# A written-out order of 1281 jobs, ordered anew, with other first loads and earlier idle matmuls

## The chip, the cores and the metric

The kernel runs on one core of one Trainium2 chip. Five engines work side by side, each through a queue of its own in order: PE (matrix products; its weight loads are listed apart, as PEld), DVE, ACT and POOL (elementwise work and copies), and SP, which only issues DMAs (ACT issues a few too). They wait for each other through semaphores. The metric is device time in microseconds; the kernel before took 269.9 us (median of three runs, 268.41 to 270.17).

## The reference

Two blocks in a row, all in float32, cut to what is computed:

```python
# attention with sketched features: q, k, v are (4 batches, 4 heads, 1088, 32), S1 and S2 are (8, 32)
a = einsum('rd,bhsd->bhsr', S1, x); b = einsum('rd,bhsd->bhsr', S2, x)
phi(x) = outer(a, b)                      # 64 features a row
kv, z = sums over s of phi(k) * v and of phi(k)
x = phi(q) @ kv / (phi(q) . z + 1e-6)     # becomes (4, 1088, 128)
# experts' attention: 4 experts, each row uses its best two
w, topk = softmax of the two largest of x @ w_gate
for e in experts:
    a = causal softmax of (x wq[e]) (x wk[e]).T / 8
    out += share of e in a row * (a @ (x wv[e]) @ wo[e])
```

S1 and S2 arrive as 64-bit floats and are turned into 32-bit ones on the chip.

## The kernel before

The program is a list of jobs (1281 of them, numbered as they are declared), each a small function that issues the instructions of one step on one engine. `Plan.run` goes through `ORDER`, a list of job numbers, and calls each; every engine gets its instructions in that order, and a letter behind a number picks the first or second engine of a job that can run on either (for a pair of idle matmuls the second choice is to leave it out). Buffers of a pool are handed out in the same order, so the list also settles which buffer a job gets, and with it whose release it waits for. No scheduler changes anything afterwards. A job waits for what it reads and for its buffer's last users.

**Start.** S1 and S2 are loaded (L235) into a tile that DVE has cleared first (job `room`, L238), decoded on DVE (L304 to L317) and copied to the other partitions by POOL, ACT and DVE (`spread`, L320). Batch 0's k comes in two halves by columns (L422, one on SP's queue and one on ACT's), its q in four pieces by head (L428), its v in four pieces (L435), which ACT copies into place (L445). DVE transposes k (L475) and q (L481). `sketch` (L510) multiplies k or q by the tables on PE; DVE transposes the result back (`back`, L514), and DVE or POOL multiplies out the 64 features (`features`, L524). `sums` (L566) is phi(k) against v. Jobs `dummy` (L249) are pairs of idle matmuls on a tile `idle` of zeros that DVE sets (L242); nobody reads what they give.

**Batch 0** then transposes q's features on PE (`turn qf`, L602), copies them (`keep qf`, L193), multiplies by the sums and divides (L628, L637). **Batches 1 to 3** do it the other way round: q's table is extended by the sums (`fifth`, L704), the features are scaled first, transposed on DVE (`turn f`, L741), and `numer` (L763) gives x already turned; ACT or DVE copies it (`keep x`), DVE turns it for the store.

**Experts.** `logits` (L814 or L820), `choose`, `shares` (L881 to L889, eight small operations on POOL) and masks fetched by DMA pick two experts a row. Per batch there are three groups of rows (of 6, 6 and 5 tiles of 64 rows). For a group PE makes the queries (L1002), DVE picks the chosen ones (L1015), and each of its tiles then runs through a chain: `score` on PE (L1040), `take` on DVE (L1052, adds the mask and finds the maximum), `exp` on ACT (L1068), `guard` (adds 1e-9; ACT L1074 or POOL L1076), `invert` on DVE (L1079), `weigh` on POOL (L1083), `turn A` on DVE (L1088). The `sum` jobs of the group (L1116) need all its tiles turned; then come copies, masks (`spread V` on POOL, L1143) and the output products (L1237, L1187, L1213). Batches overlap: batch b+1's preparation runs between batch b's groups.

Most copies can run on ACT or DVE, feature products on DVE or POOL, guards on ACT or POOL; the letters in `ORDER` choose.

The list is walked like this:

```python
for word in order:
    n, a = (int(word[:-1]), "ab".index(word[-1])) if word[-1] in "ab" else (int(word), 0)
    j = self.jobs[n]
    ...
    if j["eng"][a] != "-":
        for h in j["holds"]:
            if h not in self.where:
                self.where[h] = free[h[0]].popleft()
        j["f"](j["eng"][a])
```

Of the kernel before, what the change touches and what calls it, by code (L numbers as in the profile page):

```python
# [23 lines left out]
111 109a 107a 403 114a 113a 58 115 57 116a 407 121 404 63 122a 400 119 117 402 120a 406 405 118b 123 410 131 124 411  # L24
412 127 125 401 68 126a 132 128 135 151 152 133 11b 409 157 413a 129 415a 136 158 160 69 70 134a 130a 691 137 185 414a
184 188a 189a 153 154 155 163 156 161 416b 162a 172 690 173 14b 187 190 186 418 417 175 164a 191 159 213 688 199 408
419a 214 167 206 200 168 25b 220 215 421 207 689 420 208 422 221 209a 176 699 7b 423b 216a 192 201 138 227 193 169
425a 222 210 426 424a 174 170 202b 171b 223a 141 194 251 228 195a 250 211 252 217 6b 229 218 230a 255a 224 179 698 196
219 197 254a 427 177 253 429 180 225 198 203 71 178 212 16b 204 428 231 256 165 257 166a 72 34b 323 324 328a 296 430
226 140 435 142 232 327a 181 436 431 437 233 433a 272 329 432a 439a 13b 273 73 182 297 274 205 298 265 39b 280 281 266  # L30
258 282 275 139 694 434 259 695 326 299 267 276b 325 692 146 300b 234 438a 183a 330 301 235 277 283 284b 285 440 302
268a 702 705 703 144 278 236 148 303 237a 286 238a 240a 241 441 706a 260 288 442a 289 287 356 279 269 704a 710a 443a
242 363 261a 709a 290 364 270 271 239a 697 262 355 291 347 365 708a 461 707a 348 292a 357 5b 462 30b 701 263 696 366
693 340 367 42b 143 984 23b 244 358 293 368 27b 294 339 264 349 711 712 465 359a 18b 369a 295 150 341 463 464 145 304
305 983 350 243 370 351a 713a 466 700 306 987 371 360 352 307 342 308 147 715 467 353 444 447 361 714 354 372 309 719a
716 310b 477 718b 313a 471 311a 343a 312a 717b 314 315 362 344 476 468 720 316 990 721 331 332 480a 722 333 317 723
481a 482 479 319 334 478 724 446 448 729 483 345 320 318 491 335b 336 725 337 484 492 445 321a 485 469 543 512 346 338
542 547a 505 545 544 985 982 506 513 472 486 487a 986 488 727a 730 726a 507 473 373 374 731 375 546a 733a 450 548 376
549 732b 474 498 493 519 494a 377 475b 149 449 514 378 379 993 380 381 495 508b 520 499 515a 500 501a 382a 988 728 496
509 521 451 516 489 992 517 384a 454 734 735 989 518 510 502 383b 385b 386 387 736a 490 572 573 389 503 452 522a 737a  # L40
588 996 994 574 453 504 523 245 497 247 589 511 999 524 564 997 388 565 550 991 1000b 590 551 617 618 552 591 470 246
525 566 998a 616 557 1002b 248a 615 575 620a 558 1004a 567 755 1001b 559 592b 1003a 1006 619b 593 756 553a 457 621 757
622 758 568b 1005 594 322 759 455 460 569 765 595 554 570 576a 526 527 528 531a 648 571 760 647 577 761 530a 555 1007a
560b 532b 578 535 561 529a 649 390 632 533 581 391 631 556 580 562 658 534 563 582 655 536 656 583 650 249 459 458 623
1008 633 624 584b 634 579 585 651a 766 657 639 456 586 659 625 762 771 640 770 773 772 587 641 596 775a 774a 652 738
767 653 768 660 635b 776 777 661a 597 598 626 642 1009 1012a 662 636 654 599 663 600 392 627a 601 1013a 1010 637 664
638 643b 995 740 602a 603b 1011a 785 644 786 628 629 813 606 814 741 537 645 604a 806 607 630 605a 807 1014 778 609
539 538 739 646 1015 608 779 665 1016 780 666 540b 1017 667 1018 742 1023 808 781a 668 669 1024 32b 815 1025 787 670
671 394 816b 745 672 1019 673 792 836 21b 1021b 788b 1020b 746 674a 809a 817 541 1026a 763 1027b 837 769b 393 818 1022
675a 793 819 26b 840a 678 782 677b 612 810 611 841b 794 676a 744 783 838 752 679 1028 610 811 839 680 795b 681 799  # L50
613a 796 842 789 29b 843 1029 800 784 851 909 910 797 812 790 1031a 866 867 801 802b 791 743 1030b 852 853 914a 868
803 883 882 804 859 798 854b 858 874 884 875 805 764 860 10b 885 913b 861 876 869 844 886b 845 1049 862a 1050 911 912
877 863 915 820 846 855 878a 847a 1051 916 1052 864 848 870b 748 887 879 614 821 871 822 865 824b 823a 826a 1054 825a
849 888 889 682 942 880 872 941 36b 827 850 856 1053 933 828 683 829 881 934 949 873 750 935 925 1055 926 943 950 927
944 918 951 952 830 686 687 1135 857 945b 946 1136 928 395 917 953 954 1140b 1139b 831 1057 936 947 955a 1138 919 832
1137 920 747 754 921b 929a 1141 890 1032 937a 930 956 1142 922 891 938 923 939 685 931 948 749 1059 833 957 1182 1033
1181 834a 892 924 940 893 932 1183 1036 958 894 895 899a 684 897a 898b 1035 959 896a 753 960 961 962 963 901 1143 751
1144 19b 1145 964 965 900 1184 902 1060 966 967 1034 970b 903 1040 969b 968a 1061 1185b 971a 1150 1166 1165 1151 1041
1146b 973 1152 1158 972 974 1157 43b 1153a 1154 1173 1062 1147 1208 1167 1174 1211 1168 1209 1169a 975 1063a 1213a 9b
1186 1212a 1210 1039 1058 1175 33b 1187 1159 1170 1214 1056 1065 1066 1148 1064 1171 904 1188 1149 40b 1176 44b 906  # L60
835 1160 1069a 1177b 1037 1155 1068b 1215 1161b 1162 905 1070 1217 1045 1156 1178 907a 1172 1216 1240 1163 1179 1218
1219 1067 1180 1241 1048 1220a 1071 1164 1224 1225 1249 1233 1248 1242 1072 1221 1226 1227 908 1250 1228a 1251 1232
1252 12b 1229 1038 1243 1073 1222 1244a 1223 1234 1230 1043 1245 976 31b 1107 1108 1235 1044 977 1253 1042 1189 1246
979 1247 1109 1236a 1254a 1237 1231 1110a 1238 1190 1255 1191 1093 1086 1239 1094 1087 1192 1256 1257 980 1193 1074
28b 1100 1111 1088 1101 1095 1079 1080 1194 1258 1197a 1089b 1198a 1196b 1112 1081 1075a 1096b 1097 1082a 1259 978
1090 1260 1047 1102 1103a 1261 1262 35b 1046 1195b 1076 1077 1091 24b 1104 1263 1264 981 1083 1200 1105 1113 1098 1092
20b 1265 1199 1266 1270a 1201 1084 1267a 1106 1202 1078 1203 1204 1099 1268b 38b 1205 1085 15b 1269b 1272 1206a 1114
1115 1116 1207 1117a 1273 1271 1122 1121b 1274 1275 1119 1120a 1118 1125 1276 1123 1126 1127 1124b 1128 41b 1280 1278
1133b 1279 1277 1129a 1130b 1134a 1131b 1132a
""".split()  # L70


# [1254 lines left out]
```

## Time and profile before

| | us |
|---|---|
| median of 3 runs (lowest, highest) | 269.9 (268.41, 270.17) |
| the profiled execution | 270.48 |
| its span, first to last instruction | 268.8 |
| mean granted clock of PE in it | 0.993 |

The profile is one execution. Its page gives busy time by engine, the span in 40 slices, DMA queues, and the chain of work that ended last; the trace behind it answers for single instructions, windows and waits. Of the groups of instructions, the costliest by engine (line, engine, operation, output and inputs, size and count, then busy us and mean ns, then idle time ahead of them and who ended it):

```profile
L1083 POOL TENSOR_SCALAR w<-w,rs,sh 128x640 f32<-128x640 f32 (+16 forms) x68 | 55.6, 824 | 43.4 <-DVE rs L1079 40.2
L1068 ACT ACTIVATE w<-w,mx 128x576 f32<-128x576 f32 (+16 forms) x68 | 52.3, 770 | 58.4 <-DVE mx L1052 56.9
L1040 PE MATMUL pair<-xT,qs 128*128 128x384 f32 (+11 forms) x216 | 74.0, 480 | 0.0
```

A matmul in float32 shows as two instructions. The granted clock is recorded where it changes; ahead of the first record a window shows 1.00 whether or not that held.

### The profile page before, as it was taken

Reading aid. Unit: us, or ns where it says so; the run is one execution under the profiler, and the core shown is the slowest. Engines: PE = TensorE matmul, PEld = TensorE weight load, DVE = VectorE, ACT = ScalarE, POOL = GpSimd, SP = SyncE. Lnnn points to the kernel's source line nnn. Section 1 sums busy time; section 2 is a strip of 40 time slices with the busy share of each in tenths; the row PEclk is TensorE's granted clock in tenths of the full one; section 3 lists DMA queues with packets and bytes.
Section 4 is the critical chain, followed back from the end, with each engine's and each line's share of the span. In section 5 each row is a group of like instructions: output and inputs, shape, how many; then the busy total and the mean of one; then the engine's idle time right before and its main releaser. Section 6 shows DMA issues by size and latency. Waiting matters only on the chain.

```text
span 268.8 us, 9515 instructions
## 1 busy us (share of the span) xinstructions
PE 254.9 (95%) x3960; PEld 189.6 (71%) x3961; DVE 212.2 (79%) x550; ACT 102.6 (38%) x275; POOL 150.8 (56%) x246
## 2 busy tenths in 40 slices
PE   0889999989999999999999999999999999999994
PEld 0368576644887785876587996585789766689994
DVE  3687899997989888788999689899991379986343
ACT  2213655536622515252472323551701363354110
POOL 4276348999459944547555836166272594352741
PEclk9999999979999999999999999999999999999999
DMA  7938559990238677513441094402670458321012
GB/s 160 188 68 195 115 115 215 186 165 11 45 83 167 165 131 118 154 30 98 108 67 29 6 229 87 111 4 50 149 140 20 99 133 204 54 50 30 5 32 54
DMA packets 87739, 27.36 MB, mean 102 GB/s; under 512 B 58576, under 2 KB 87056, under 8 KB 87696
## 3 DMA queue, kind: packets, MB, share of 16 engines
q1 hardware_dynamic: 85184, 26.11, 48.1%
q10 hardware_dynamic: 2512, 0.64, 1.2%
q8 instruction: 31, 0.51, 0.9%
q14 instruction: 12, 0.10, 0.2%
HBM read 22.22 MB, written 4.52 MB: 100 GB/s over the span
## 4 chain that ended last, share of the span: by engine, by line
PE 77%; DVE 1%; issue 0%; DVEq 0%
PE pair L1116 28%; PE pair L1040 23%; PE pair L1002 8%; PE pair L1237 7%; PE pair L1187 3%; PE pair L763 2%; PE pair L566 2%; PE pair L510 2%; PE pair L1213 1%; PE pair L814 1%; DVE fp L741 0%; DVE w L514 0%; PE pair L704 0%; PE pair L698 0%; DVE ob L193 0%
## 5 line engine op out<-in xcount | busy, mean ns | idle before, releaser
L1083 POOL TENSOR_SCALAR w<-w,rs,sh 128x640 f32<-128x640 f32 (+16 forms) x68 | 55.6, 824 | 43.4 <-DVE rs L1079 40.2
L1068 ACT ACTIVATE w<-w,mx 128x576 f32<-128x576 f32 (+16 forms) x68 | 52.3, 770 | 58.4 <-DVE mx L1052 56.9
L1040 PE MATMUL pair<-xT,qs 128*128 128x384 f32 (+11 forms) x216 | 74.0, 480 | 0.0
L1052 DVE CUSTOM_DVE_ANT_0 w<-pair,mask 128x768 f32<-128x768 f32 (+14 forms) x68 | 48.2, 726 | 17.6 <-PE pair L1040 16.2
L1040 PEld LDWEIGHTS pair<-xT,qs 128*128 128x128 f32 x216 | 38.3, 190 | 25.4 <-issue 10.9
L1088 DVE STREAM_TRANSPOSE AT<-w 128x384 f32<-128x384 f32 (+15 forms) x68 | 50.4, 758 | 1.3 <-POOL w L1083 1.1
L1143 POOL TENSOR_TENSOR agg<-agg,mb 128x768 f32<-128x768 f32 (+1 forms) x22 | 34.1, 1559 | 20.2 <-ACT agg L193 7.0
L1116 PEld LDWEIGHTS pair<-AT,xra 32*128 32x128 f32 x1136 | 41.7, 185 | 4.4 <-issue 2.4
L1116 PE MATMUL pair<-AT,xra 32*128 32x160 f32 (+5 forms) x1136 | 44.7, 303 | 0.0
L1002 PE MATMUL pair<-xT,Mq 128*128 128x384 f32 (+1 forms) x96 | 34.3, 475 | 0.0
L193 ACT COPY agg<-pair 128x384 f32<-128x384 f32 (+1 forms) x31 | 13.4, 467 | 42.4 <-PE pair L1116 39.9
L524 POOL TENSOR_TENSOR fp<-w 128x576 f32<-128x576 f32 (+1 forms) x21 | 24.8, 1198 | 8.3 <-DVE w L514 8.0
L1116 PE MATMUL pair<-AT,xrb 32*128 32x160 f32 (+5 forms) x752 | 27.8, 288 | 0.0
L1116 PEld LDWEIGHTS pair<-AT,xrb 32*128 32x128 f32 x752 | 26.6, 185 | 1.5 <-issue 1.4
L1002 PEld LDWEIGHTS pair<-xT,Mq 128*128 128x128 f32 x96 | 17.2, 190 | 10.2 <-issue 2.5
L1015 DVE COPY_PREDICATED qs<-mb,pair 128x768 f32<-128x768 uint16 (+1 forms) x24 | 23.1, 964 | 0.8 <-ACT qs L193 0.4
L1237 PEld LDWEIGHTS pair<-Mo,agg 128*128 128x128 f32 x168 | 20.5, 192 | 3.1 <-issue 0.5
L1237 PE MATMUL pair<-Mo,agg 128*128 128x128 f32 x168 | 21.2, 277 | 0.0
L1076 POOL TENSOR_SCALAR rs<-zs 128x1 f32<-128x1 f32 x27 | 6.7, 249 | 17.9 <-ACT w L1068 13.4
L193 DVE COPY agg<-pair 128x384 f32<-128x384 f32 (+1 forms) x15 | 7.6, 516 | 10.8 <-ACT agg L193 5.9
L514 DVE STREAM_TRANSPOSE w<-pair 128x576 f32<-128x576 f32 (+2 forms) x18 | 12.1, 696 | 4.1 <-PE pair L510 3.8
L1139 DVE COPY_PREDICATED agg<-mb,pair 128x384 f32<-128x384 uint16 (+1 forms) x24 | 12.8, 547 | 1.1 <-ACT agg L193 1.0
(169 smaller groups left out, 292.5 us busy)
## 6 DMA issues: line engine op xcount, KB each, us to landing
xra<-xd SPq DMA_DIRECT2D x16, 192.0 KB, 4.4
xrb<-xd SPq DMA_DIRECT2D x16, 192.0 KB, 4.6
xrc<-xd SPq DMA_DIRECT2D x16, 160.0 KB, 4.1
mb<-md SPq DMA_DIRECT2D x4, 576.0 KB, 5.8
mb<-md SPq DMA_DIRECT2D x4, 480.0 KB, 5.0
mb<-md SPq DMA_DIRECT2D x6, 288.0 KB, 5.2
in<-in_k_dram SPq DMA_DIRECT2D x12, 136.0 KB, 3.9
in<-in_q_dram SPq DMA_DIRECT2D x3, 544.0 KB, 6.1
```

Source lines behind the costliest of these rows:

```text
L193: (nc.scalar.copy if eng == "ACT" else VEC[eng].tensor_copy)(o, i)
L524: VEC[e].tensor_tensor(out=f, in0=a[:, :, None, R : 2 * R].to_broadcast([128, j1 - j0, R, R]), in1=a[:, :, 0:R, None].to_broadcast([128, j ...
L1002: nc.tensor.matmul(plan[ps[x]][:, y, 0:w], Mq[:, ((1, 2), (0, 3))[x][y]], plan[xT][:, 64 * t0 : 64 * t1], start=True, stop=True)
L1015: nc.vector.copy_predicated(chosen(), rows(c), rows(plan[ps[x]]))
L1040: nc.tensor.matmul(plan[p][:, y, 0 : c1 - c0], plan[qs][:, 128 * t : 128 * t + 128], plan[xT][:, c0:c1], start=True, stop=True)
L1052: nc.vector.tensor_tensor_reduce(out=o, in0=src, in1=msk, scale=-1.0, scalar=mx[:, b, i, x - 1 : x] if x else 3e38, op0=ALU.add, op1=ALU.m ...
L1068: nc.scalar.activation(out=a, in_=a, func=ACTF.Exp, bias=mx[:, b, i, last : last + 1], scale=-1.0, accum_out=zs[:, b, i : i + 1])
L1083: nc.gpsimd.tensor_scalar(out=a, in0=a, scalar1=rs[:, b, i : i + 1], scalar2=plan[("sh", b)][:, i : i + 1], op0=ALU.mult, op1=ALU.mult)
L1088: nc.vector.transpose(dst[:, 0 : keys // 32, t], plan[A][:, 0:keys].rearrange("p (j s) -> p j s", s=32))
L1116: nc.tensor.matmul(plan[Vk[g // 2]][:, g % 2, lo : 32 * nt], plan[(f"xr{j // 12}", b)][rows, j % 12], a[rows, j, lo:], start=(j == 0), sto ...
L1143: nc.gpsimd.tensor_tensor(out=a, in0=a, in1=plan[mb][:, 2 * x : 2 * x + 2, 0:w], op=ALU.mult)
L1237: nc.tensor.matmul(plan[p][0:m, 0, 128 * x : 128 * x + 128], plan[agg][:, e, 128 * x : 128 * x + m], Mo[:, e], start=(e == 0), stop=(e == ...
```

## The change

Only the list `ORDER` differs. Its first and last lines before, with `-`, and after, with `+`:

```diff
 ORDER = """
-0 80 2 74 76 3 48 46 75 87 1 4 78 51 86 81 83 45 37a 54 79 49 77 82 50 90 91 60 84a 92 59 8a 22a 53 56 17a 52 95a 61
-85a 89 100 88 62b 102 101 108a 97 110a 99 65 66 64 96b 112 397 396 105a 398 94b 93b 106b 98 399 47 67a 104a 55 103a
...
+0 1 2 3 4 74 75 76 77 78 21a 45 80 83 23a 13a 79 48 29a 87 86 81 50 46 60 5a 51 30a 24a 82 49 52 90 27a 92 89 14a 58
+91 59 95a 61 96b 397 93b 399 88 53 398 62a 396 100 19a 102 97 94a 101 110a 108a 109b 84a 85a 107a 99 112 111 54 105b
+113a 117 64 106b 98 103a 406 118a 121 55 56 104b 114a 65 119 407 66 122a 400 115 404 120a 67a 63 410 68 57 401 116a 70
...
-1133b 1279 1277 1129a 1130b 1134a 1131b 1132a
+1127 1280 1128 1133a 1134b 1131b 1129b 1132b 1130a 43a
 """.split()
```

In words, engine by engine where the prediction needs it (the numbers are jobs):

- **SP** before: v's first piece (80), S1 (2), k's first half (74), two pieces of q (76, 78), v's others (81, 83, then 82 behind a weight load). After: S1, k's first half, two pieces of q, then v's four, one weight load (52), and batch 1's k loads (397, 399, 398, 396) with a second weight load (53) among them. ACT's queue before: S2 (3), k's second half (75), the table load and its activation (4), two pieces of q. After: S2, the table load and activation, k's second half, the two pieces of q.
- **PE** before: one pair of idle matmuls (37), the first sketch (90, of k), three pairs. After: seven pairs (21, 23, 13, 29, 5, 30, 24), the first sketch, two pairs (27, 14), `repeat S2` (61), the first sketch of q (100), one pair (19), and one pair (43) as the last thing on PE. No real matmul job is added or dropped.
- **DVE**: the tile `idle` is set right after `room` instead of between the two transpositions of k (87, 86). The copies of S2 (62) and of one part of q's features (118) go to ACT, three feature products of q (109, 105, 104) and one of batch 1's k (416) to POOL, one of batch 0's k (94) from POOL to DVE.
- **Later**, all engines take their jobs in another order throughout. The last `sum` job of batch 0 no longer stands directly ahead of batch 2's `numer`: three score jobs of batch 1 (tiles 2 and 9) come between. In batch 2, POOL takes the shares of batch 3 (job `shares 3.0`) between the first and the second `weigh` of the last group instead of behind that group. Of the 68 guards, 31 run on POOL instead of 27, and some copies trade ACT for DVE and back.

More of the change, by code (lines that the diff above doesn't have):

```diff
@@ L27 @@
[L27 to L66, printed above, removed]
@@ new lines @@
+1053 878b 864 916 392 1052 879 682 827 880 825a 865 872 824a 934 828 850 888 1059 830 933 1054 925 826a 935 936 942
+889 941 873 1060 943 944 949 950 937a 926 683 829 39b 917 1136 1135 927 938 918 1140a 952 881 951 1139b 1137 945a 953
+928 929b 1055 1138 749 1057 754 919 833 920 752 930 1141 954 921a 1142 939 832 831 1181 1061 1182 946 940 834a 947
+955a 890 835 891 1032 892 893 956 894 1034 685 931 957 948 895 958 1183 1184 922 897a 687 932 923 1035 924 896b 900
+959 1185a 899a 898a 901 902 960 1150 753 1033 1151 1173 1174 1165 1152 1166 1175 903 1143 1144 961 962 963 964 1186
@@ new lines @@
+1245 977 1246 1231 1237 1191 1072 1247 1222 1223 1041 980 1046 1073 1238 1100 1239 1086 1101 1074 1109 1087 1256 979
+1045 1192 1257 1193 1093 1079 1080 1094 1194 1081 1258 1095 1096b 42b 1259 1102 1260 1075b 1196b 1110b 1103b 1076
+1197a 1261 684 1104 1198a 1195b 1200 1111 1105 1112 1088 1106 1262 978 1263 1201 1264 1082a 1083 1097 1113 1265 1199
+1084 1085 1202 1077 1266 1098 1078 686 1089b 1090 1091 981 1269a 1099 1267a 1092 1205 1270a 1271 1203 1204 1268b 1114
+1272 1115 1206b 1116 1274 1117a 1122 1273 1121a 1118 1119 1120b 1275 1276 1123 1207 1279 1277 1278 1125 1126 1124b
```

39 lines of the change are left out of this document (34 added, 5 removed).

## The prediction, made before the result was known

> **What bounds the kernel now.** I read the busy times and the forty slices first, then the chain of waits in order of time, then busy times by window, and last the timeline of the first 24 us and of the places where the chain leaves PE.
>
> The page's busy times, and the slices of PE:
> ```profile
> span 268.8 us, 9515 instructions
> PE 254.9 (95%) x3960; PEld 189.6 (71%) x3961; DVE 212.2 (79%) x550; ACT 102.6 (38%) x275; POOL 150.8 (56%) x246
> ...
> PE   0889999989999999999999999999999999999994
> ```
> PE is without work at the start, a little in slices 1, 2 and 8, and at the end; otherwise it is full. So there are two kinds of gain: an earlier start, and PE's few waits. The chain of waits (start, length, what) reaches back to 55 us, and is PE's own from there to the last copy but for these places:
> ```profile
> 55.10 1.10 DVE fp L741
> ...
> 57.10 3.17 PE pair L763 x46
> ...
> 102.20 1.30 PE pair L763 x23
> ...
> 103.68 0.74 PE pair L763 x15
> ...
> 165.08 1.48 PE pair L763 x38
> ```
> L763 is `numer`, the product of q's features with k's sums, once for each of batches 1, 2 and 3. The same work takes 1.48 us at 165, 2.22 at 102 and 3.17 at 57. Windows (length, then busy us of PE, PEld, DVE, ACT, POOL, then clock, DMA share and GB/s) say why the first is slow:
> ```profile
> 56.00:57.00 1.00, 0.12 (x3) 0.01 (x1) 1.00 (x3) 0.87 (x3) 1.00 (x2) 0.99 1.22 139
> 57.00:58.00 1.00, 0.90 (x18) 0.43 (x32) 1.00 (x3) 1.00 (x3) 1.00 (x2) 0.50 1.21 152
> ```
> PE stands idle for 0.9 us at 56, DVE and POOL being full, and then has a granted clock of 0.50. That stop costs 0.9 + (3.17 - 1.48) = 2.6 us.
>
> Now the start (timeline: start, length, engine, line, what, idle before it and who ended it):
> ```profile
> 0.79 0.39 SPq L435 DMA_DIRECT2D w<-in_v_dram  x1
> ...
> 1.00 0.58 ACTq L235 DMA_DIRECT2D w<-in_S_dram  x1
> ...
> 1.24 0.35 SPq L235 DMA_DIRECT2D w<-in_S_dram  x1
> ...
> 1.64 0.36 SPq L422 DMA_DIRECT2D in<-in_k_dram  x1
> ...
> 2.10 0.37 ACTq L428 DMA_DIRECT2D in<-in_q_dram  x1
> ...
> 3.32 0.20 ACT L245 ACTIVATE warm<-warm 128x1 f32<-128x1 f32 x1
> ...
> 3.80 0.17 DVE L304 TENSOR_SCALAR w<-w 32x32 int32<-32x32 int32 x1 [2.81 <-DMA w<-in_S_dram]
> ...
> 6.32 0.78 DVE L475 STREAM_TRANSPOSE in<-in 128x576 f32<-128x576 f32 x1 [0.79 <-DMA in<-in_k_dram]
> ...
> 7.11 0.27 DVE L242 MEMSET idle<- 128x256 uint32 x1
> ...
> 7.44 1.03 PE L249 MATMUL pair<-idle 128*128 128x512 bf16 x2 [7.44 <-DVE idle L242]
> ...
> 8.40 2.59 PE L510 MATMUL pair<-in,SK 32*32 32x288 f32 x64
> ...
> 10.90 1.45 DVE L514 STREAM_TRANSPOSE w<-pair 128x576 f32<-128x576 f32 x2 [2.57 <-PE pair L510]
> ```
> The first sketch (8.40) waits for k's halves, not for the tables: the tables are decoded by 5.53 (6.32 less 0.79 of idle), then DVE waits for k.
>
> **The change part by part.** Both kernels hold the same jobs; the order in which each engine takes them differs, and some copies, products and 1e-9 additions change engine.
>
> *First loads.* The table on ACT's queue is first in its queue today, and DVE waits for both, so "tables first" can bring at most 1.24 - 1.00 = 0.24 us, in a place with 0.79 us of idle behind it: nothing. What counts is that v's first piece no longer runs ahead of k. Its size (list of loads: count, KB each, us to landing), and the rate in the window when k was landing:
> ```profile
> w<-in_v_dram SPq DMA_DIRECT2D x3, 144.0 KB, 3.4
> ```
> ```profile
> 4.00:6.00 2.00, 0.00 (x0) 0.00 (x0) 1.47 (x13) 0.23 (x1) 0.25 (x2) 1.00 1.18 281
> ```
> 0.147 MB at 281 GB/s is 0.5 us; I take 0.4, as SP issues k only 0.24 earlier. On ACT, k's half now stands behind the table load and its activation. Today q's load stands there, and went out at 2.10, ahead of the activation at 3.32, so I add nothing (bound: it goes out 1.3 us later, at the activation, and the gain of k is lost). The idle tile's memset (0.27) leaves the stretch between the two transpositions of k for DVE's wait at the front. So the first sketch starts at 8.40 - 0.4 - 0.3 = 7.7: **-0.7 us** (0 to -0.9).
>
> *Idle matmuls.* Seven pairs instead of one stand ahead of the first sketch, and start once the idle tile is set, at about 1.3 us. Fourteen at 1.03 / 2 = 0.5 us would end at 8.5; at a doubled clock for the last part, before 7.7. The first sketch against the same shape in batch 1 (ns: min, median, max; first and last start):
> ```profile
> L510 PE MATMUL pair<-in,SK x64: 679/682/684, 8.4 to 10.3; 32*32 32x288 f32 x64
> L510 PE MATMUL pair<-in,SK x64: 401/401/425, 23.2 to 24.4; 32*32 32x288 f32 x64
> ```
> 2.59 us against 24.4 + 0.4 - 23.2 = 1.6: the first runs at the slow clock. With idle matmuls from 1.3 to 7.7 I expect the fast one: **-1.0 us** (+0.8, if slow idle matmuls end at 8.5 and the sketch is slow too, to -1.0). The Trainium skill, "TensorE: Matmul & The Clock Gate", Part 1, holds that the clock doubles after one busy window of about 3.4 us in a free-running count, and that this ramp is worth under 1% of a usual kernel's span; an estimate from its figures has the clock up between 4.7 and 8.1 us, so it is not sure of the first sketch, and would by itself allow at most half of 3.4, 1.7 us. No row here shows the moment at which the clock rises; the slow first sketch, 1 to 3 us behind the first idle matmul, agrees. Three more pairs stand behind the first sketch and one at the very end; the first three lie in gaps where PE waits for DVE, the last beside the final stores: nothing, or 0.9 us if PE were late there.
>
> *DVE up to the second batch.* From 10.90 to about 20 DVE is nearly full, and PE waits for it. The order takes work from it:
> ```profile
> 11.83 2.14 ACT L193 COPY vp<-w 96x1152 f32<-96x1152 f32 x2 [6.04 <-DMA w<-in_v_dram]
> ...
> 12.38 0.76 DVE L524 TENSOR_TENSOR fp<-w 128x576 f32<-128x576 f32 x1
> 12.43 4.02 POOL L524 TENSOR_TENSOR fp<-w 128x576 f32<-128x576 f32 x3 [4.50 <-DVE w L514]
> ...
> 14.35 0.42 DVE L193 COPY S2r<-pair 64x64 f32<-64x64 f32 x2
> ...
> 16.42 1.02 DVE L524 TENSOR_TENSOR fp<-w 128x384 f32<-128x384 f32 x2
> ...
> 17.77 0.36 DVE L524 TENSOR_TENSOR fp<-w 128x192 f32<-128x192 f32 x1
> ```
> The copy of S2 goes to ACT (-0.42), one long and two short q products to POOL (-0.51, -0.72), one k product comes from POOL (+0.76): **-0.9 us** (0 to -0.9). POOL's cover is the 4.5 us of idle ahead of its products; if it were gone, what it has more (by a k product's 4.02 / 3 no more than 1.3) would be late for the transpositions of q's features. v's pieces go out behind q's now: the same engines carry the same bytes ahead of ACT's copy of v (11.83), and were that 2 us late, it would end at 16.0, before POOL's k products do today (16.5), which the same sums need: nothing. Batch 1's k loads reuse the tile that the first sketch reads and go out as it ends, earlier with it; one weight load stands among the four: nothing, or the 1 us by which DVE might wait for them.
>
> *The stop at 55 to 60.* What PE waited for is DVE: the last transposition of q's features (L741), then one of a sketch. DVE's work in the window that ends as that transposition starts, and one copy in it:
> ```profile
> 0.00:55.02 55.02, 45.72 (x797) 30.30 (x798) 42.90 (x140) 22.29 (x58) 31.84 (x81) 1.00 0.81 155
> ```
> ```profile
> 22.52 0.69 DVE L193 COPY fp<-pair 128x512 f32<-128x512 f32 x1 [1.22 <-ACT fp L193]
> ```
> Of these 42.9 us the new order takes out, beside what is counted above, that copy (0.69, to ACT) and one k product (0.76 by the row of its shape, to POOL): 1.4 us that PE does not gain, since no real matmul crosses `numer` of batch 1 either way. DVE is 1.4 us ahead of today's meeting, where PE's idle was 0.9. So the idle goes, and the half clock with it: -2.6. What is late next is POOL's last q product of batch 1 (full at 56 to 57 today); it also has one k product and two short ones more, early. I take **-2.2 us** (0 to -2.6).
>
> *Batch 2's numer.* 2.22 us against 1.48, because today it directly follows the last sums whose buffers it takes. Now a score in batch 1 and two more stand between: **-0.6 us** (0 to -0.7).
>
> *New waits.* Everywhere else PE's excess over its best rate is below 0.5 us a place, so a new order can only lose there. Twelve groups of scores are each followed by a chain over DVE, ACT, DVE, POOL, DVE to the group's sums. For the last of batch 2 the chain ends at 200.44 + 1.30 and the sums start at 203.1 (rows below): 1.3 us of room, typical. I allow **+1.5 us** (0 to +6).
>
> Sum: -0.7 - 1.0 - 0.9 - 2.2 - 0.6 + 1.5 = -3.9. The profiled execution took 270.48 us, 1.7 around its span; that gives 266.6. The median of the three runs, 269.9, is 0.6 below that execution, so I forecast **266.0**.
>
> **The rivals.** *The stop only moves* (0.22): another meeting of DVE or POOL with PE costs the 2.8 us that leave at 55 and 102, and only the start's 2.6 less 1.5 remain: 268.8; for it speaks that DVE is nearly as full after 130 as at 40. *The first sketch still runs slow* (0.15): the first idle pair ran at 7.44 and matmuls were still slow at 10.3, 2.9 us later, while mine have 6.4 us: so rather not. It takes back 1.0 (1.8 at most): 267.0. The Trainium skill's window rule ("TensorE: Matmul & The Clock Gate", Part 1) gives this too where its count falls late. *Slower* (0.13): POOL's queue in batch 2. Today the shares of batch 3 (eight small POOL operations) stand behind that batch's last group; now they stand inside it, ahead of four of its five weighings:
> ```profile
> 212.75 0.24 POOL L881 TENSOR_TENSOR ch<-ch,c 128x18 f32<-128x18 f32 x1
> ...
> 214.57 0.21 POOL L889 TENSOR_TENSOR ch<-ch 128x9 f32<-128x9 f32 x1
> ```
> ```profile
> 195.29 3.23 POOL L1083 TENSOR_SCALAR w<-w,rs,sh 128x832 f32<-128x832 f32 x3 [1.48 <-DVE rs L1079]
> ```
> ```profile
> 200.44 1.30 DVE L1088 STREAM_TRANSPOSE AT<-w 128x1088 f32<-128x1088 f32 x1
> ...
> 203.09 3.10 PEld L1116 LDWEIGHTS pair<-AT,xra 32*128 32x128 f32 x86
> ```
> ```profile
> 190.00:200.00 10.00, 10.00 (x126) 7.84 (x129) 9.92 (x18) 4.10 (x10) 5.79 (x7) 1.00 0.74 135
> ```
> The shares take 2.0 us from first to last, four weighings 4 x 3.23 / 3 = 4.3. DVE is full there and takes its queue in order; if it stood still through all of that, 6.3 us less the 1.3 of room would stop PE, and the half clock behind such a stop adds 1.7: 266.0 + 6.7 = 272.7. It decides from 6.3 us of standstill on, and reaches 274 if the fifth weighing waits too; against it, POOL is busy for only 5.8 of 10 us. *Forecast* (0.50), its own range 263.2 to 267.6.
>
> **The numbers.** About 1% is what a measurement of this kernel tells from no change (its runs lie 0.7% apart). Faster than 267.2: 0.9 of the forecast, a quarter of the moved stop (it may be smaller), half of the slow sketch: 0.45 + 0.05 + 0.08 = 0.58. Slower than 272.6: the POOL rival, 0.13. Between: 0.29. The range 263.2 to 271.0 leaves out the POOL rival and the forecast's best 0.07.
>
> **What would show it.** Right: first sketch at 7.5 to 8.0 with matmuls of 400 ns; DVE's first turn of a sketch near 9.3; no clock of 0.50 between 13 us and the end; `numer` near 1.5 us in all three batches; PE's end about 4 us earlier. Wrong: k's ACT half landing behind the activation; a PE idle of 1 us with half clock anywhere later; DVE idle ahead of the transpositions of A in batch 2; or the gain of the first 20 us used up by a full DVE before 55.

## The result, and the profile after

| | before | after |
|---|---|---|
| median of 16 runs (lowest, highest), us | 269.43 (268.41, 272.67) | 266.66 (264.34, 268.54) |
| the profiled execution, us | 270.48 | 264.85 |
| its span, us | 268.8 | 262.9 |
| its granted clock | 0.993 | 1.000 |

The ratio is 0.987 (95% interval 0.984 to 0.990): 1.3% faster, inside the range and 0.7 us from the 266.0 forecast. How that number comes about is another matter. The runs of the changed kernel form two groups: seven at a granted clock of 0.998 or 1.000 and 264.34 to 265.08 us, seven near 0.994 and 266.5 to 268.4, with two at 0.987 above them; with nine of sixteen runs outside the first group, the median lies between the two fastest of the second. A stretch of 3.41 us at half clock takes 0.6% off the mean clock of a run, so 0.994 is one such stretch. It would cost 1.7 us if PE were busy all through. The old kernel has the two groups too: beside the first experiments ten runs at 0.999 or 1.000, median 268.94, and eight at 0.991 to 0.994, median 270.12. Its groups lie 1.2 us apart, those of the changed kernel 2.4. The old kernel's profiled execution was of the second group. Below, "at full clock" means the median of a kernel's runs at 0.997 or more: 268.9 before (268.8 to 269.0 on three chips, 269.7 on a fourth), **264.85 after, a difference of 4.1 us**. The clocks of the table's sixteen old runs are not on record, so this difference is one between different sets of runs. A few executions at far lower clocks, e4's profiled one among them, are left out.

The page of the changed kernel: span, busy times, PE by slices and the granted clock.

```profile
span 262.9 us, 9532 instructions
PE 256.6 (98%) x3975; PEld 191.4 (73%) x3975; DVE 211.5 (80%) x544; ACT 102.1 (39%) x273; POOL 153.8 (59%) x254
...
PE   7999999999999999999999999999999999999995
...
PEclk9999999999999999999999999999999999999999
```

Busy times barely move (DVE 212.2 to 211.5 us, POOL 150.8 to 153.8). Above all PE's first slices changed. The start, as a timeline (start, length, engine, line, what, idle before it):

```profile
1.00 0.38 SPq L235 DMA_DIRECT2D w<-in_S_dram  x1
...
1.31 4.72 PE L249 MATMUL pair<-idle 128*128 128x512 bf16 x14 [1.31 <-DVE idle L242]
...
1.70 0.37 ACTq L422 DMA_DIRECT2D in<-in_k_dram  x1
...
2.85 0.17 DVE L304 TENSOR_SCALAR w<-w 32x32 int32<-32x32 int32 x1 [1.60 <-DMA w<-in_S_dram]
...
2.93 0.20 ACT L245 ACTIVATE warm<-warm 128x1 f32<-128x1 f32 x1
...
5.37 1.37 DVE L475 STREAM_TRANSPOSE in<-in 128x576 f32<-128x576 f32 x2 [0.76 <-DMA in<-in_k_dram]
...
6.79 1.61 PE L510 MATMUL pair<-in,SK 32*32 32x288 f32 x64 [0.76 <-DVE in L475]
...
8.46 0.78 DVE L514 STREAM_TRANSPOSE w<-pair 128x576 f32<-128x576 f32 x1 [1.51 <-PE pair L510]
```

The tables are decoded 0.95 us earlier (2.85 against 3.80), k is turned 0.95 earlier (5.37 against 6.32), the first sketch starts 1.6 earlier and takes 1.61 us in place of 2.59, and DVE has it back 2.4 earlier. The clock's first record stands at 4.43 us in this trace, at 12.61 in the old one.

How long the lead lasts is read from when PE first and last starts each line (ns min, median, max; first and last start). Before:

```profile
L566 PE MATMUL pair<-vp,fp x288: 190/223/244, 16.8 to 118.4; 128*64 128x33 f32 x144
L602 PE MATMUL pair<-ident,fp x18: 272/273/329, 20.2 to 22.1; 128*128 128x128 f32 x18
L1116 PE MATMUL pair<-AT,xra x1136: 243/294/425, 52.0 to 260.0; 32*128 32x160 f32 x76, 32*128 32x192 f32 x71, 32*128 32x128 f32 x12, 32*128 32x96 f32 x11
L763 PE MATMUL pair<-fp,kvr x192: 372/402/685, 57.1 to 166.2; 32*32 32x288 f32 x96, 32*32 32x256 f32 x96
L1213 PE MATMUL pair<-Mo,agg x24: 272/275/294, 262.5 to 265.1; 128*128 128x128 f32 x24
```

After:

```profile
L566 PE MATMUL pair<-vp,fp x288: 215/223/245, 12.9 to 114.5; 128*64 128x33 f32 x144
L602 PE MATMUL pair<-ident,fp x18: 272/272/328, 16.0 to 18.6; 128*128 128x128 f32 x18
L1116 PE MATMUL pair<-AT,xra x1136: 243/294/425, 48.1 to 254.0; 32*128 32x160 f32 x75, 32*128 32x192 f32 x70, 32*128 32x128 f32 x15, 32*128 32x96 f32 x11
L763 PE MATMUL pair<-fp,kvr x192: 373/400/429, 52.6 to 158.5; 32*32 32x288 f32 x96, 32*32 32x256 f32 x96
L1213 PE MATMUL pair<-Mo,agg x24: 273/275/275, 256.5 to 259.1; 128*128 128x128 f32 x24
```

PE leads by 3.9 us at the first sums (L566), 4.2 at the turn of q's features (L602), 3.9 at the experts' first sums (L1116), 4.5 at batch 1's `numer` (L763). From there to the last products (L1213) the old trace takes 205.4 us and the new one 203.9, but the old one has its half-clock stretch in that part. The traces of e2 and e3 (below), which have the old list there and no such stretch, take 203.8 and 204.4, so the rest is level to about 0.5 us. Nearly all that is gained at full clock stands at 57 us, most of it at 17.

Waits of PE over 0.2 us in the changed kernel, those of its weight loads left out (line, what it waited for; us, times, longest):

```profile
PE pair L249 <- DVE idle L242: 1.3, 1, 1.3
PE pair L510 <- DVE in L475: 0.8, 1, 0.8
PE pair L566 <- issue: 0.6, 1, 0.6
```

### The profile page after: what moved, and what is told of

It is laid out like the page before. It is cut to its first block, busy times and chain, and to the rows that moved or that the text cites. A ratio compares the mean times of both kernels' runs of the same rounds, so it can differ in the third digit from the quotient of the medians.

```text
span 262.9 us, 9532 instructions
## 1 busy us (share of the span) xinstructions
PE 256.6 (98%) x3975; PEld 191.4 (73%) x3975; DVE 211.5 (80%) x544; ACT 102.1 (39%) x273; POOL 153.8 (59%) x254
## 4 chain that ended last, share of the span: by engine, by line
PE 91%; DMA 4%; DVE 2%; issue 1%; SPq 0%; ACTq 0%; ACT 0%; DVEq 0%
PE pair L1116 30%; PE pair L1040 24%; PE pair L1002 11%; PE pair L1237 7%; PE pair L510 4%; PE pair L566 4%; PE pair L1187 3%; DMA xra<-xd 3%; PE pair L763 2%; DMA in<-in_k_dram 1%; PE pair L1213 1%; PE pair L628 1%; DVE xT L193 1%; PE pair L602 1%; DVE in L475 1%
## 5 line engine op out<-in xcount | busy, mean ns | idle before, releaser
L1068 ACT ACTIVATE w<-w,mx 128x320 f32<-128x320 f32 (+14 forms) x68 | 52.5, 772 | 60.5 <-DVE mx L1052 59.3
L1083 POOL TENSOR_SCALAR w<-w,rs,sh 128x576 f32<-128x576 f32 (+14 forms) x68 | 56.2, 835 | 33.2 <-DVE rs L1079 32.3
L1052 DVE CUSTOM_DVE_ANT_0 w<-pair,mask 128x448 f32<-128x448 f32 (+14 forms) x68 | 48.8, 725 | 9.5 <-PE pair L1040 9.1
L1088 DVE STREAM_TRANSPOSE AT<-w 128x192 f32<-128x192 f32 (+16 forms) x68 | 50.9, 761 | 4.1 <-POOL w L1083 4.0
L1116 PEld LDWEIGHTS pair<-AT,xra 32*128 32x128 f32 x1136 | 42.0, 185 | 5.6 <-issue 2.8
L1116 PE MATMUL pair<-AT,xra 32*128 32x192 f32 (+5 forms) x1136 | 45.5, 303 | 0.2 <-DMA xra<-xd 0.2
L1002 PE MATMUL pair<-xT,Mq 128*128 128x384 f32 (+1 forms) x96 | 35.1, 479 | 0.0
L524 POOL TENSOR_TENSOR fp<-w 128x576 f32<-128x576 f32 (+2 forms) x25 | 27.6, 1124 | 9.2 <-DVE w L514 6.7
L193 ACT COPY agg<-pair 128x384 f32<-128x384 f32 (+1 forms) x34 | 14.2, 464 | 43.4 <-PE pair L1116 41.0
L1116 PE MATMUL pair<-AT,xrb 32*128 32x160 f32 (+5 forms) x752 | 27.3, 288 | 0.0
L1116 PEld LDWEIGHTS pair<-AT,xrb 32*128 32x128 f32 x752 | 26.1, 185 | 0.9 <-issue 0.8
L193 DVE COPY agg<-pair 128x384 f32<-128x384 f32 (+1 forms) x12 | 6.2, 525 | 9.4 <-PE pair L1116 6.7
```

What stands on the lines that cost most here:

```text
L193: (nc.scalar.copy if eng == "ACT" else VEC[eng].tensor_copy)(o, i)
L524: VEC[e].tensor_tensor(out=f, in0=a[:, :, None, R : 2 * R].to_broadcast([128, j1 - j0, R, R]), in1=a[:, :, 0:R, None].to_broadcast([128, j ...
L1002: nc.tensor.matmul(plan[ps[x]][:, y, 0:w], Mq[:, ((1, 2), (0, 3))[x][y]], plan[xT][:, 64 * t0 : 64 * t1], start=True, stop=True)
L1052: nc.vector.tensor_tensor_reduce(out=o, in0=src, in1=msk, scale=-1.0, scalar=mx[:, b, i, x - 1 : x] if x else 3e38, op0=ALU.add, op1=ALU.m ...
L1068: nc.scalar.activation(out=a, in_=a, func=ACTF.Exp, bias=mx[:, b, i, last : last + 1], scale=-1.0, accum_out=zs[:, b, i : i + 1])
L1083: nc.gpsimd.tensor_scalar(out=a, in0=a, scalar1=rs[:, b, i : i + 1], scalar2=plan[("sh", b)][:, i : i + 1], op0=ALU.mult, op1=ALU.mult)
```

## The experiments

Each edits only the list. The jobs computed are the same in all of them; idle matmuls are the only work added or left out.

**Where the gain lies: h1 and h2.** The two lists joined at the first turn of q's features, new start with old rest (h1) and the reverse (h2). The seams:

```diff
-85a 89 100 88 62b 102 101 108a 97 110a 99 65 66 64 96b 112 397 396 105a 398 94b 93b 106b 98 399 47 67a 104a 55 103a
+91 59 95a 61 96b 397 93b 399 88 53 398 62a 396 100 19a 102 97 94a 101 110a 108a 109b 84a 85a 107a 99 112 111 54 105b
+113a 37a 8a 22a 56 17a 65 66 64 106b 98 47 67a 104a 55 103a 403 114a 115 57 116a 407 121 404 63 122a 400 119 117 402
...
-111 109a 107a 403 114a 113a 58 115 57 116a 407 121 404 63 122a 400 119 117 402 120a 406 405 118b 123 410 131 124 411
+111 109a 107a 403 114a 113a 58 21a 23a 13a 29a 5a 30a 24a 27a 14a 19a 117 406 118a 121 119 407 122a 400 115 404 120a
```

> The changed list up to the first turn of the query features (PE's work up to 16.0 us of the changed kernel's trace), then all other jobs in the old list's order, on the old list's engines. Theory A (the gains add up, place by place): PE is 3.9 us ahead when the first sketches are done (turn of k at 16.07 against 19.94) and keeps that lead, and the old order's stop (PE idle 0.9 us for DVE's turn back, a window at half clock, batch 1's numer at 3.17 us) stays, some 4 us earlier than 56: 269.4 - 3.9 = 265.5 us. Theory B (the old stop was DVE's lateness and takes the lead back): PE comes 4 us earlier, DVE does not, the stop grows: 267.5 to 269.4. Theory C (the stop was itself a result of the slow start and goes with it): 269.4 - 3.9 - 2.2 = 263.3, with no row of PE waiting for L514 at batch 1's numer.

> The old list up to the first turn of the query features, then all other jobs in the changed list's order and on its engines. Theory A: the start as before (first sketch near 8.4 at 2.6 us, turn of k near 19.9), then no stop at batch 1's numer: 269.4 - 2.2 = 267.2 us. Theory B (all of the gain is the start's): 269.4. Theory C (the changed list behind the start is itself slower, its waits hidden so far by the lead): over 270.

Measured: h1 268.07 us (ratio 0.996, 0.994 to 0.998), 267.43 at full clock; h2 271.8 (1.007, 1.003 to 1.011), all ten runs at full clock. Both joints have a flaw that I had overlooked: the idle pairs of the second list, not yet used, all fall at the seam, where PE has other work to do. The timelines of h1 and of h2 there:

```profile
16.05 1.90 PE L249 MATMUL pair<-idle 128*128 128x512 bf16 x7
```

```profile
19.97 4.49 PE L249 MATMUL pair<-idle 128*128 128x512 bf16 x19
```

Less 1.90, h1 comes to 265.5, a gain of 3.4 at full clock (theory A's figure, though that was reckoned from 269.4); less 4.49, h2 comes to 267.3, a gain of 1.6. These are upper bounds, since other engines caught up while PE ran idle matmuls, and together they are more than the 4.1 there is. h1 still shows the old stop (PE waited 0.8 us at L763), h2 does not. So, if the two parts simply add, the start holds 2.5 to 3.4 us, and the rest of the list 0.7 to 1.6.

**The idle matmuls: e1 and e2.** e1 leaves the seven early pairs out of the changed kernel, e2 puts them into the old one:

```diff
-0 1 2 3 4 74 75 76 77 78 21a 45 80 83 23a 13a 79 48 29a 87 86 81 50 46 60 5a 51 30a 24a 82 49 52 90 27a 92 89 14a 58
+0 1 2 3 4 74 75 76 77 78 21b 45 80 83 23b 13b 79 48 29b 87 86 81 50 46 60 5b 51 30b 24b 82 49 52 90 27a 92 89 14a 58
...
-0 80 2 74 76 3 48 46 75 87 1 4 78 51 86 81 83 45 37a 54 79 49 77 82 50 90 91 60 84a 92 59 8a 22a 53 56 17a 52 95a 61
+0 1 80 2 74 76 3 48 46 75 87 4 21a 23a 13a 29a 5a 30a 24a 78 51 86 81 83 45 37b 54 79 49 77 82 50 90 91 60 84a 92 59
```

> The changed kernel without the seven pairs of idle matmuls ahead of the first sketch (14 of its instructions; the later pairs stay). Theory A (the clock): first sketch starts at 6.8 as with them but runs at half clock, 2.6 us in place of 1.61, later stages all 1.0 us later: 266.7 + 1.0 = 267.7 us, clock records from about 11. Theory B (DVE has other work until 9.3 anyway): first turn back later by under 0.3 us, time within 0.3 of 266.7. Theory C (the clock comes later still, since pauses among the sketches keep it low): +2 us or more.

> The old kernel with one edit: its idle tile is set first of all, and seven pairs of idle matmuls stand ahead of its first sketch in place of one. Theory A: first sketch still starts at 8.4 but takes 1.6 us in place of 2.59, and DVE's first turn back starts at 9.9 in place of 10.9: 269.4 - 1.0 = 268.4 us. Theory B (the lead is lost again at DVE between 11 and 20, or at the stop at 56): 269.4, within 0.3. Theory C (the idle matmuls end near 6.0, and the pause until 8.4 drops the clock again): first sketch still 2.6, 269.4.

Measured: e2 takes 266.84 us (0.990, 0.983 to 0.996), four runs all at full clock: **2.1 us less than the old kernel at full clock**, from one edit, twice what I had expected of it. e1 is unsteady: of four runs two took 265.95 and 266.35, 1.3 above the changed kernel at full clock, the other two 270.5 and 270.9. All four have a mean granted clock of 1.000, which counts only from the first clock record on, and neither of the last two was profiled, so the cause of their 4.5 us more stays open. e1's profiled run (266.35) shows the slow first sketch (matmuls of 684 ns, as in the old kernel). Where e2's second microsecond comes from is read in PE's start of the sums, here in e2:

```profile
12.77 2.01 PE L510 MATMUL pair<-in,SK 32*32 32x192 f32 x128 [0.93 <-DVE in L481]
...
15.53 2.29 PE L566 MATMUL pair<-vp,fp 128*64 128x33 f32 x72
17.89 2.36 PE L602 MATMUL pair<-ident,fp 128*128 128x128 f32 x17
```

and in the old kernel:

```profile
16.78 0.54 PE L566 MATMUL pair<-vp,fp 128*64 128x33 f32 x11
18.35 1.95 PE L566 MATMUL pair<-vp,fp 128*64 128x33 f32 x61 [1.03 <-issue]
20.23 0.98 PE L602 MATMUL pair<-ident,fp 128*128 128x128 f32 x7
```

The sums start 1.25 us earlier. Of this, 0.25 is the idle tile's memset, which no longer stands between k's two transpositions (the first sketch starts at 8.15 in e2, 8.40 before); 1.0 is the sketch. Then a pause of 1.03 us inside the sums, for which the profile names no releaser, is gone: 2.3 at L602. The last section gives the signs that PE waits for its code there.

**The loads: e3 and l1.** The changed order of the first loads in the old list, and the old one in the changed list:

```diff
-0 80 2 74 76 3 48 46 75 87 1 4 78 51 86 81 83 45 37a 54 79 49 77 82 50 90 91 60 84a 92 59 8a 22a 53 56 17a 52 95a 61
+0 2 3 74 75 76 48 46 77 87 1 4 78 51 86 80 83 45 37a 54 79 49 81 82 50 90 91 60 84a 92 59 8a 22a 53 56 17a 52 95a 61
...
-0 1 2 3 4 74 75 76 77 78 21a 45 80 83 23a 13a 79 48 29a 87 86 81 50 46 60 5a 51 30a 24a 82 49 52 90 27a 92 89 14a 58
+0 1 80 2 4 74 76 3 75 78 21a 45 81 83 23a 13a 79 48 29a 87 86 77 50 46 60 5a 51 30a 24a 82 49 52 90 27a 92 89 14a 58
```

> The old kernel with one edit: its first twelve loads stand in the changed list's order (the two sketch tables, k's two halves, q, then v). Single runs of the old kernel at a granted clock of 1.000 have lain near 268.9 us, those at 0.994 near 270, so times are compared at 1.000. Theory A: the table is decoded 0.95 us earlier as in the changed kernel, k's half is turned 0.95 earlier, the first sketch starts at 7.5 in place of 8.4 but still at half clock: 268.9 - 0.9 = 268.0 us. Theory B (my first sum: tables first is worth nothing, k gains 0.4 to 0.5): 268.4. Theory C (v comes late and keeps the next stages waiting): 269 or more.

> The changed kernel with its first twelve loads in the old list's order. Theory A (the loads are worth in the new list what e3 showed in the old one, 0.4 us): 264.9 + 0.4 = 265.3 us at a clock of 1.000. Theory B (with PE's clock up, the first sketch waits for k's turn alone, so the full 0.95 us of the earlier landing counts): 265.9. Theory C (v early is worth as much as k early): 264.9.

Measured: e3 268.92 us (0.9975, 0.9953 to 0.9997), at full clock 268.64 against 269.0: -0.4. l1 266.80 (0.989, 0.986 to 0.992), at full clock 265.70 against the changed kernel's 264.85: 0.85. Whether the loads are worth more in the new list is not shown: l1's five runs at full clock spread from 265.07 to 267.27, and the intervals of l1 and the changed kernel overlap. k's first transposition starts at 5.73 in e3 and 5.84 in e5 (below), against 6.32 before and 5.37 in the changed kernel, so the 0.95 us of that one trace is the most that was seen.

**Both together: e5.** e2's and e3's edits in the old list:

```diff
-0 80 2 74 76 3 48 46 75 87 1 4 78 51 86 81 83 45 37a 54 79 49 77 82 50 90 91 60 84a 92 59 8a 22a 53 56 17a 52 95a 61
+0 1 2 3 74 75 76 48 46 77 87 4 21a 23a 13a 29a 5a 30a 24a 78 51 86 80 83 45 37b 54 79 49 81 82 50 90 91 60 84a 92 59
```

> The old kernel with two edits: seven pairs of idle matmuls at once (as in e2) and the first loads in the changed list's order (as in e3); the rest of the list and all engines as before. Theory A (the two add, and the rest of the new list is worth what is left): e2's 266.84 - 0.95 = 265.9 us. Theory B (these two are the whole change): 264.9, the changed kernel's time at a clock of 1.000. Theory C (the earlier k is lost at the next wait, for DVE's turns): 266.8 as e2.

Measured: 267.24 us (0.992, 0.988 to 0.995), at full clock 266.69 (three runs): theory C, hardly better than e2. What is left to the changed kernel, 1.8 us, is the rest of the list.

**The engines: e4 and e8.** e4 gives jobs 62, 118 (copies), 109, 105, 104 and 94 (products) their old engines in the changed list; e8 gives them their new ones in e5's list:

```diff
-91 59 95a 61 96b 397 93b 399 88 53 398 62a 396 100 19a 102 97 94a 101 110a 108a 109b 84a 85a 107a 99 112 111 54 105b
-113a 117 64 106b 98 103a 406 118a 121 55 56 104b 114a 65 119 407 66 122a 400 115 404 120a 67a 63 410 68 57 401 116a 70
+91 59 95a 61 96b 397 93b 399 88 53 398 62b 396 100 19a 102 97 94b 101 110a 108a 109a 84a 85a 107a 99 112 111 54 105a
+113a 117 64 106b 98 103a 406 118b 121 55 56 104a 114a 65 119 407 66 122a 400 115 404 120a 67a 63 410 68 57 401 116a 70
...
-8a 22a 53 56 17a 52 95a 61 85a 89 100 88 62b 102 101 108a 97 110a 99 65 66 64 96b 112 397 396 105a 398 94b 93b 106b 98
+8a 22a 53 56 17a 52 95a 61 85a 89 100 88 62a 102 101 108a 97 110a 99 65 66 64 96b 112 397 396 105b 398 94a 93b 106b 98
...
```

> The changed kernel with the six early jobs back on their old engines (copies of S2 and of one turned query piece from ScalarE back to DVE, three of the query's products from GpSimd back to DVE, the second quarter of k's turn back to GpSimd's or the other engine of the old list). Theory A (DVE is what the start waits for): turn of the query features 0.9 us later, 264.9 + 0.9 = 265.8 us at a clock of 1.000. Theory B (the new order, not the engines, gave the lead at 16 us): within 0.3 of 264.9. Theory C (DVE is late from there on, and PE waits at batch 1's numer again): +1.8 or more, with a row of PE waiting for L514.

> The old kernel with three edits: the early idle matmuls and the first loads' order (as in e5), and the six early jobs on the changed list's engines (the reverse of e4's edit). The rest of the list stands in the old order. Theory A (the engines are worth in the old order what they were in the new one, and the new order itself nothing): e5's 266.6 us at a clock of 1.000 less e4's 1.4 = 265.2 us. Theory B (only the new order makes room for GpSimd's slower products): 266.6 or more, as e5. Theory C (the old order with them is better than the changed kernel): below 264.7.

Measured: e4 267.42 us (0.991, 0.988 to 0.995), at full clock 266.26 (three runs, 265.78 to 267.16): 1.4 slower than the changed kernel. e8 is slower than the old kernel: 272.08 (1.011, 1.006 to 1.015), every run at 0.975 to 0.981. Its timeline shows a new wait:

```profile
12.34 2.14 ACT L193 COPY vp<-w 96x1152 f32<-96x1152 f32 x2 [7.68 <-DMA w<-in_v_dram]
...
14.51 0.42 ACT L193 COPY S2r<-pair 64x64 f32<-64x64 f32 x2
...
14.98 1.18 PE L510 MATMUL pair<-in,SK 32*32 32x96 f32 x48 [1.06 <-ACT S2r L193]
```

In the old order the copy of S2 stands behind ACT's 2.14 us copy of v, and the sketch of q waits for it; in the changed kernel it runs at 10.03, ahead of that copy (10.49). After these pauses come three windows at half clock (13.98 to 24.22 us), at most 5.1 us. Without those e8 would be near 267 (an estimate, 272.08 - 5.1), no better than e5. So DVE's relief is worth something in the new order, and in the old one these six jobs together gain nothing. Which of the six matters was not taken apart.

**The stop at 55 to 60: e6.** Batch 1's `numer` two score jobs later in the old list:

```diff
-268a 702 705 703 144 278 236 148 303 237a 286 238a 240a 241 441 706a 260 288 442a 289 287 356 279 269 704a 710a 443a
+268a 702 705 703 144 278 236 148 303 237a 286 238a 240a 241 706a 260 288 289 441 442a 287 356 279 269 704a 710a 443a
```

> The old kernel with one edit: batch 1's numer stands two score jobs later in PE's list, so that the 0.98 us that PE idled at 56.1 for DVE's turn back are filled with scores. Theory A (a real stop): 268.9 - 0.9 = 268.0 us at a clock of 1.000, and no run at 0.994, since the half-clock window came of this pause. Theory B (the pause was only DVE's lateness and comes back at the next job that waits for DVE): 268.9, runs at 0.994 as often as before. Theory C (0.994 has nothing to do with this pause): 268.0 and 269.5 side by side.

Measured: 270.24 us (1.0026, 1.0002 to 1.0050), at full clock 270.2: slower by 1.2. PE's timeline:

```profile
57.05 1.45 PE L1040 MATMUL pair<-xT,qs 128*128 128x352 f32 x4 [0.33 <-DVE w L514]
58.43 2.13 PE L763 MATMUL pair<-fp,kvr 32*32 32x288 f32 x64
61.89 1.56 PE L1040 MATMUL pair<-xT,qs 128*128 128x512 f32 x3 [1.33 <-ACT xT L193]
```

The pause ahead of the `numer` shrank to 0.33 us, but a new one of 1.33 came behind it: the two scores that had run while ACT copied the result now stand ahead, and PE waits for the copy. So e6 traded one wait for a longer one, near theory B; it does not tell whether DVE's lateness could be filled with other work. But only one of ten runs has a half-clock window (0.993, the others 0.997 or more), against 17 of 31 of the old kernel beside it.

**More idle matmuls: c1 and c2.** One more pair ahead of the first sketch (both), and one ahead of batch 1's `numer` (c1):

```diff
-0 1 2 3 4 74 75 76 77 78 21a 45 80 83 23a 13a 79 48 29a 87 86 81 50 46 60 5a 51 30a 24a 82 49 52 90 27a 92 89 14a 58
+0 1 2 3 4 74 75 76 77 78 21a 45 80 83 23a 13a 79 48 29a 87 86 81 50 46 60 5a 51 30a 24a 44a 82 49 52 90 27a 92 89 14a
...
-236 277 283 262 299 440 705 238a 239a 284b 703 278 263 300b 279 237a 706a 269 709a 270 301 302 242 441 241 285 264 288
+236 277 283 262 299 440 705 238a 239a 284b 703 278 263 300b 279 237a 706a 269 709a 270 301 302 242 12a 441 241 285 264
```

> The changed kernel with two more pairs of idle matmuls: one between the seventh pair and the first sketch, in a pause of 0.76 us, and one just ahead of batch 1's numer, where PE pauses for 0.5 us. Theory A (runs at 0.994 come of a window of low PE activity in the sums and the pause ahead of batch 1's numer, as in the profiled old kernel): all runs at 1.000, median 265.0 us, 1.6 below the changed kernel's 266.66. Theory B (the window falls elsewhere): runs at 0.994 as often as before (7 to 9 of 16), median 266.7. Theory C (the pairs delay the first sketch or the numer): +0.3 to +0.9 in every run.

> The changed kernel with one more pair of idle matmuls, between the seventh pair and the first sketch (c1 without its pair ahead of batch 1's numer). Theory A (c1's pair ahead of the numer cost its 0.4 us and did nothing else; the pair ahead of the sketch filled the pause there and moved the code-loading pause of 0.62 us off the sums): 264.5 us at a clock of 1.000, and one run in six or fewer at 0.994, since the half-clock windows of the changed kernel come of the sketches between 10 and 16 us: median 264.6. Theory B (the windows come of batch 1's numer, and c1's pair there had kept them away): runs at 0.994 in half of the cases, median 265.5 to 266.5. Theory C (c1's 1.000 runs were chance, one pair does nothing): median 266.7 as the changed kernel.

Measured: c1 265.30 us (0.987, 0.983 to 0.990), five of six runs at full clock, 265.13. **c2 264.31 us (0.977, 0.975 to 0.979), five runs at full clock, 264.12, the best version of all**: on its chip the old kernel took 270.08, and the changed kernel's interval (0.984 to 0.990) lies above c2's. c2's list of PE's waits no longer has the row of L566, and its timeline has the sums in one piece:

```profile
13.17 2.29 PE L566 MATMUL pair<-vp,fp 128*64 128x33 f32 x72
15.42 0.65 PE L602 MATMUL pair<-ident,fp 128*128 128x128 f32 x4
```

Its first sketch starts 0.3 later (7.1 against 6.8), and yet L602 0.6 earlier. Ten of eleven runs of c1 and c2 are at full clock, against seven of sixteen of the changed kernel; that points to the start as the place of its half-clock windows. h2 agrees, which has the old start with the new rest and all ten runs at full clock, and so does l1's trace, where half clock begins at 15.44 us; but the changed kernel's own trace has none.

## Why the prediction was right

The forecast came out right in part by luck: errors of opposite sign nearly cancel. At full clock the start gave 1.3 to 1.6 us more than its terms, the stop at 55 to 60 about 1.5 less, and behind it the lists are level to 0.5 us where the terms for batch 2's `numer` and new waits say 0.9 lost. The difference of the medians is 2.8 us, not 3.9; that the forecast is only 0.7 off is because it starts from 269.9, the median of three runs, 0.5 above that of the sixteen.

- **First loads, -0.7.** The term holds 0.4 for the loads, as e3 measured in the old list, and 0.3 for the memset, of which e2 shows 0.25. It is wrong in a part. "Tables first is worth nothing" failed: DVE's wait for the tables ends 0.95 earlier, likely because v's piece ahead of them cost more than the 0.24 us of issue that I counted. k's half on ACT was issued at 1.70, ahead of the activation at 2.93: that bound did not come.
- **Idle matmuls, -1.0.** The first sketch runs at full clock, 1.61 us, and the rival in which it stays slow falls. The sketch's own 1.0 is right, but the edit is worth more: of the 2.1 in the old list (e2) 0.25 is the memset, and most of the rest goes with the pause of 1.03 us in the sums, which the prediction does not have. The clock's first record stands at 4.1 to 7.2 us in the eight traces at full speed that have the early idle matmuls, and their first sketch starts at 6.5 to 8.2 (in e8 at 7.15 and 7.78, with 0.6 to spare). The Trainium skill, "TensorE: Matmul & The Clock Gate", Part 1, gives the ramp's cost as under 1% of a usual span; this agrees: the sketch's 1.0 us is 0.4% of 268.9, and all of e2's 2.1 is 0.8%.
- **DVE up to the second batch, -0.9.** 1.4 by e4, of about the right size, but bound to the new order, as e8 suggests; I had not seen this as a condition. DVE's first turn came at 8.46, not 9.3.
- **The stop, -2.2.** This step failed. PE's pause ahead of `numer` did go (0.98 us before, under 0.2 now). But `numer` did not fall from 3.17 to 1.48 with it, because the half clock was not all that made it slow. In e2, with the old list there and at full clock, and in the changed kernel:

```profile
55.09 2.33 PE L763 MATMUL pair<-fp,kvr 32*32 32x288 f32 x64 [1.00 <-DVE w L514]
55.75 1.16 PEld L763 LDWEIGHTS pair<-fp,kvr 32*32 32x32 f32 x60 [0.53 <-DVE w L514]
```

```profile
52.57 2.18 PE L763 MATMUL pair<-fp,kvr 32*32 32x288 f32 x64
53.23 1.01 PEld L763 LDWEIGHTS pair<-fp,kvr 32*32 32x32 f32 x60 [0.52 <-DVE w L514]
```

After four weights the loads wait 0.5 us for DVE's second turn back, in both lists; so of the 1.7 us that the prediction priced as half clock only 0.8 was (3.17 against 2.33), and the rest stays. Only the pause was the new list's to win, and the lead grows by 0.6 to `numer`'s start and by 0.15 within it. The half clock itself is something that about half of the old kernel's runs do not have and half of the changed kernel's runs have in their turn. I should have asked whether the profiled run, 0.6 above the median, was like the others. "The stop only moves" falls too, but e6 shows how easily a pause there moves.

- **Batch 2's `numer`, -0.6, and new waits, +1.5.** `numer` of batch 2 takes 1.57 us now, near its best; but it takes 1.68 in e2 and 2.04 in e3, which have the old order, so its place behind the last sums does not by itself explain today's 2.22. Of the 1.5 for new waits some 0.5 or less was needed, as the lists are level behind 57 us.
- **The POOL rival** did not come: no wait of PE for POOL is in the list of waits above 0.2 us.

By medians the start's extra gain stood in for a clock gain that did not exist; at full clock the change is worth 4.1 us where these steps, without the 1.7 for half clock, said 2.2.

## What to carry to other kernels

Before a stop in one profiled execution is priced, the granted clock of that execution is to be held against that of other runs: half-clock windows come and go between runs of one list, though the list changes how often (none in h2's ten runs, some in all four of e8's). A slow stretch should also be compared with the same one at full clock, as waits can hide in it. Matmuls on zeros that start with the program are the cheapest edit here: in the old list they bring 2.1 us, half as much as the whole change. Moving work to a freer engine can fail where its queue has no room at that place (S2's copy, 0.42 us, behind a copy of 2.14).

## What the runs showed of the hardware

**Half clock can follow a window with PE idle for a quarter of it.** The clock's changes lie 3.413 us apart or at multiples of it within a trace (12.61 and 56.98 before: 13 times 3.413). These are such windows in the old kernel, in e5 (two), in e8, in l1 and in e2 (length, then busy us of PE, PEld, DVE, ACT, POOL, clock, DMA share, GB/s):

```profile
53.57:56.98 3.41, 2.55 (x90) 1.88 (x82) 2.74 (x7) 0.85 (x3) 3.23 (x6) 1.00 1.44 150
16.02:19.44 3.42, 2.39 (x57) 2.11 (x56) 3.32 (x9) 0.80 (x1) 2.00 (x3) 1.00 0.01 1
```

```profile
52.14:55.56 3.42, 2.43 (x91) 1.47 (x65) 3.16 (x5) 1.90 (x5) 3.30 (x5) 1.00 1.02 159
4.36:7.77 3.41, 1.78 (x24) 0.69 (x38) 1.74 (x4) 0.23 (x1) 1.63 (x8) 1.00 1.32 223
```

```profile
10.56:13.98 3.42, 2.34 (x86) 1.61 (x84) 2.47 (x5) 1.62 (x2) 1.74 (x1) 1.00 1.36 182
```

```profile
12.02:15.44 3.42, 2.30 (x99) 1.69 (x91) 3.42 (x8) 1.39 (x2) 2.48 (x2) 1.00 0.76 134
```

```profile
54.06:57.47 3.41, 2.41 (x66) 1.25 (x66) 3.41 (x6) 1.92 (x6) 3.41 (x5) 1.00 1.09 167
```

The old kernel's first row and the first rows of e5, e8 and l1 were each followed by half clock, with PE idle for 0.86 to 1.12 us of the window (25 to 33%). The old kernel's second row and e2's, with PE idle for 1.03 and 1.00 us, were not, and neither was e5's second, with 1.63. So half clock can come after a window in which PE was busy for two thirds to three quarters, and idle time alone does not decide; what else does stays open. The Trainium skill, "TensorE: Matmul & The Clock Gate", "Why this matters for your kernels", asks that PE not pause for more than about 3 us; these traces differ, since half clock came after windows with a third of that idle.

**PE seems to wait for its code.** In eight traces (before, after, h1, h2, e1, e3, e6, l1) PE pauses for 0.3 to 1.1 us after about its 448th instruction, whatever the job, and the profile names only "issue". The trace's DMA packets point to a cause: the first packet of 16 KB on the larger of the profile's two instruction queues starts at 15.95 us before, 11.29 after, 12.45 in e2 and 10.07 in c2, and PE goes on 2.40 and 2.60 us later in the first two, 2.4 to 3.0 in all eight. In e2 and c2 it started at PE's 179th and 178th instruction, and PE came to the place late enough; before and after it started at the 412th and 303rd. What decides the start was not settled. The Trainium skill, "Runtime: NRT & Kernel Launch", "Instruction fetch mechanics", calls the crossing of such a 16 KiB block mostly hidden; if that is what these pauses are, PE lost up to 1.1 us by it here.
